# One core of T5 attention with a three-way maxout FFN: the left-over keys' band loaded by DMA, a spread moved to VectorE, bands and an FFN block reordered

## The chip, the cores and the metric

The kernel runs on one core of a Trainium2 chip. The metric is the device time of one execution in microseconds (us); less is better. The core has a matrix engine (TensorE, PE in the profile, with its weight loads as PEld), VectorE (DVE), ScalarE (ACT), GpSimd (POOL), a queue engine that only issues transfers (SyncE, SP), and 16 DMA engines. Each engine works through its own queue strictly in the order in which the program put it there. A semaphore makes an instruction wait for one on another engine, and everything behind it in its queue then waits too.

## The reference

Attention over 8 batches of 8 heads, 576 positions of 64 numbers, with a bias that depends on the distance of query and key alone; then an FFN whose hidden layer is the largest of three products.

```python
scores = scale * np.matmul(q, k.transpose(0, 1, 3, 2))
n = np.abs(pos[:, None] - pos[None, :])
bucket = np.where(n < half, n, large)            # large: logarithmic in n
scores = scores + bias_table[bucket].transpose(2, 0, 1)[None]
attn = softmax(scores)                           # over the keys
x = np.matmul(attn, v).transpose(0, 2, 1, 3).reshape(B * S, H * D)
h = np.maximum(np.maximum(x @ w1, x @ w2), x @ w3)
return h @ w_out                                 # 4608 x 512, w: 512 x 768
```

## The kernel before

Work goes by batch and, within a batch, by pair of heads (`hp` 0 to 3). For a pair, TensorE makes the scores with the keys on the partitions (tiles `sc`); ScalarE takes the exponential into `e4` (512 keys in 4 tiles, by 512 queries). The 64 left-over keys (positions 512 to 575; tile `sct`) and the 64 left-over queries (`scq`) go into a second tile, `el`. The bias is applied behind the exponential, as a factor: far from the diagonal it is constant and drops out in the division, so only a band around the diagonal is multiplied, on VectorE (`times_band`, `times_band_pair`, `times_band_left`, `times_bandt`). The factors stand in `hank`, 128 partitions by 8 heads by 384, where row p is the same vector shifted by p: a DMA with overlapping rows reads it from `w_dr`, a small vector per head in DRAM (`load_hank`, L340). The band is read backwards along the queries. For the left-over keys the rows of `hank` do not serve as they are, since the two heads of a pair share the 128 partitions: `bandt` holds their 192 factors per pair, made from `hank` by two GpSimd copies that also turn the order round (`make_bandt`, L356).

TensorE then multiplies `e4` and `el` by the values (tile `a`, two halves of the queries); VectorE divides by the sums (`quotients`: RECIPROCAL `rd`, then the product into `x_sb`). In batch one of eight, TensorE transposes `x_sb` (`xp`) and ScalarE copies it to `xT` (`x_transposes`), of which the FFN reads all four pairs' parts.

The batch that comes first (b = 0) is written out in two loops over `hp`. The first loop makes the scores of the first half of the queries for all pairs. The second makes the other half, and puts the weighted sums, quotients, bands and left-over work of earlier steps between them. `bands(hp)` multiplies the band of pair `hp`'s first half: one double and one single multiply. Behind these comes a general loop over (b, hp) from (1, 0) on.

The second batch (b = 1) is loaded in another layout, packed, into the end of `xT`, two heads first (`load_second`). `spread_packed(hp, engine)` copies a pair from there to `q_sb` and `k_sb`, one copy each; `second_transposes` then lets TensorE transpose them (10 transposes, `tp`), VectorE copies the queries to qT and ScalarE the keys to kT. For pair 0 the spread is done by GpSimd, for pairs 1 to 3 by VectorE.

The FFN is filler for TensorE. `add_ffn(t0, n)` appends the work on n tokens as a list of portions to `pending`, and `fill(target, ...)` takes portions from there while their sizes add up to no more than the target. For the first 256 tokens there are three blocks: `first(0)` (4), then `first(1)` with `second(0)` (8), then `second(1)` (4), then `first(2)` with `second(2)` (8). A `first` is 8 matmuls with the first weights and a ScalarE copy to `hT` (L418); a `second` is 8 matmuls with the second weights and a VectorE maximum (L427). The thirds follow later, deferred.

Of the kernel before, what the change touches and what calls it, by code (L numbers as in the profile page):

```python
# [12 lines left out]
ALU = mybir.AluOpType  # L13
# [26 lines left out]
def kernel(  # L40
# [12 lines left out]
    nc = tc.nc  # L53
    B, H, S, D = q.shape
# [5 lines left out]
    HP = H // 2  # L60
    QS = 2 * P
# [10 lines left out]
    BAND = 3 * P  # L72
    HALF = 2 * P - 1
    WL = 2 * HALF + 1
# [17 lines left out]
    inorder = tc.keep_in_program_order  # L92
# [19 lines left out]
    def tr(*args):  # L112
        inorder(nc.tensor.transpose(*args))  # L113
# [8 lines left out]
    def act_copy(out_, in_):  # L122
        return inorder(nc.scalar.activation(out=out_, in_=in_, func=ACTF.Copy))

    def dve_copy(out_, in_):
        return inorder(nc.vector.tensor_copy(out_, in_))  # L126
# [122 lines left out]
    def spread_packed(hp, eng):  # L249
        h = slice(2 * hp, 2 * hp + 2)  # L250
        for dst, src in zip(batch[1], (q_1, k_1)):
            inorder(eng.tensor_copy(dst[:, :, h, :], src[:, h].rearrange("p h t d -> p t h d")))
# [38 lines left out]
    for vv in range(single, NB):  # L291
# [5 lines left out]
        out=pick[:, 0:NW], in0=pick[:, 0:NW], scalar1=pick[:, NW:], scalar2=None, op0=ALU.is_equal,  # L297
# [38 lines left out]
    w_dr = dram.tile([H, WL], BF16, name="w_dr")  # L336
    hank = const.tile([P, H, BAND], BF16, name="hank")

    def load_hank(h0, h1):
        inorder(nc.sync.dma_start(  # L340
            out=hank[:, h0:h1, :],
            in_=bass.AP(
                tensor=w_dr.tensor, offset=w_dr.offset + h0 * WL,
                ap=[[1, P], [WL, h1 - h0], [1, BAND]],
            ),
        ))
# [2 lines left out]

    bandt = const.tile([P, HP, 192], BF16, name="bandt")  # L350

    def make_bandt():
        for par in range(2):
            r = slice(64 * par, 64 * par + 64)
            c = BAND // 2 - 64 * par
            inorder(nc.gpsimd.tensor_copy(bandt[r, :, :], hank[r, par::2, c : c + 192][:, :, ::-1]))  # L356

# [334 lines left out]
    def add_ffn(t0, nt, last=False):  # L694
        portions, left = ffn(t0, nt, last)
        portions[0] = rest + portions[0]
        rest[:] = left
        pending.extend((sum(n for n, _ in p), [fn for _, fn in p]) for p in portions)
# [10 lines left out]
    def fill(target, *hooks):  # L709

        groups, spent, hooks = [], 0, list(hooks)
        while pending and (not groups or spent + pending[0][0] <= target):
            n, fns = pending.pop(0)
            spent += n
            groups += [fn for fn in fns if fn]
        for j, group in enumerate(groups):
            while hooks and (j == len(groups) - 1 or j > 0 and len(hooks) > len(groups) - 1 - j):
                hooks.pop(0)()
            group()
        for hook in hooks:  # L720
            hook()
# [183 lines left out]

    def times_bandt(hp, el):
        return inorder(nc.vector.tensor_tensor(
            out=el[:, S - 192 : S], in0=el[:, S - 192 : S], in1=bandt[:, hp, :], op=ALU.mult
        ))

    def left_queries(hp, qT, kT, el):
# [113 lines left out]
    def x_transposes(hp, half):  # L1025

        xp = ps_f.tile([P, 2 * CH], BF16, tag="ff", name="xp")
        lo, hi = (0, QS) if half == 0 else (QS, S)
        for q in range(lo // P, -(-hi // P))[::-1]:
            c = min(P * q, S - P) - lo  # L1030
            tr(xp[:, c : c + P], x_sb[0][:, q, P * hp : P * hp + P], ident[:])
        act_copy(xT[:, hp, lo:hi], xp[:, 0 : hi - lo])
# [8 lines left out]
    def next_late():  # L1041
        return late.pop(0)() if late else (lambda: None)
# [13 lines left out]
    on_zeros(warm[:, 0:CH])  # L1056
    for h0 in (0, KT):
        load_hank(h0, h0 + KT)
    dve_copy(batch[0][0][:, 0:2, 2:KT, :], q32[:, :, 2:KT, :])
    cast_keys(1)  # L1060
    w_bf = [const.tile([P, DCH, d_ff], BF16, name=f"w{i}_bf") for i in range(3)]
# [10 lines left out]
    def load_second():  # L1072
        for h0, h1 in ((0, 2), (2, H)):
            load_packed(k, h0, h1, k_1)
            load_packed(q, h0, h1, q_1)
            if h0 == 0:
                load_q_tail(1)
                load_tail(k, 1, 0, H, k_diag)
                load_w(1)
                make_bandt()  # L1080
        spread_packed(0, nc.gpsimd)
        load_v(1, 0, H)
        load_w(2)

# [3 lines left out]
    def bands(hp):  # L1088
        times_band_pair(hp, first_e[hp], 0, 0)
        times_band(hp, first_e[hp], 2, 0, QS, inorder)  # L1090
# [9 lines left out]
    for hp in range(HP):  # L1100
        qT, kT = (x[:, hp, :] for x in qk[0])
        e4, el = e_tiles()
# [29 lines left out]
    for hp in range(HP):  # L1132
        qT, kT = (x[:, hp, :] for x in qk[0])
        if begun:
            e4, el = begun.pop()
            more_transposes(hp + 1)
            scores(qT, kT, e4, 1, 2)
        else:
            e4, el = e_tiles()
            visit(qT, kT, e4, [(1, 0), (1, 2)], (lambda: more_transposes(hp + 1)) if hp + 1 < HP else None)  # L1140

        def keys():
            left_keys(hp, qT, kT, el, QS, S)

        def queries():
            left_queries(hp, qT, kT, el)

        def late_bands(hp=hp, e4=e4):
            times_band(hp, e4, 1, QS, QM, inorder)
            times_band_pair(hp, e4, 2, QS)  # L1150

        if hp == 0:
            keys()
        if hp == 1:
            x_transposes(0, 0)
        quotients = next_late()
        if hp < 2:
            quotients()
            if hp == 0:
                bands(2)  # L1160
            else:
                behind.pop()()
                keys()
            queries()
            if hp == 1:
                x_transposes(1, 0)
            else:
                begun.append(e_tiles())
                scores(*(x[:, 1, :] for x in qk[0]), begun[0][0], 1, 0)
            quotients = next_late()  # L1170
            quotients()
            if hp == 0:
                bands(3)
            behind.append(lambda late_bands=late_bands, hp=hp, el=el: (late_bands(), products(hp, el)))
        else:
            if behind:
                behind.pop()()
            if hp == 3:
                quotients()
                add_ffn(0, QS)  # L1180
                fill(8)
            keys()
            if hp == 2:
                quotients()
            queries()
            late_bands()
            if hp == 2:
                x_transposes(2, 0)
                x_transposes(3, 0)
            else:  # L1190
                begin_qk(2)
                x_transposes(0, 1)
                fill(8, lambda: second_transposes(qk[1], 0))
            products(hp, el)
        late.append(lambda hp=hp, e4=e4, el=el: attend(0, hp, e4, el, 1))
# [15 lines left out]
    for b, hp in [(b, hp) for b in range(1, B) for hp in range(HP)]:  # L1211
# [3 lines left out]
        e4, el = begun[0] if begun else e_tiles()  # L1215
# [215 lines left out]
```

## Time and profile before

| quantity | before |
|---|---|
| time, median of 3 runs | 307.47 us (306.84 to 308.44) |
| profiled execution, its own time | 307.46 us |
| its span in the profile | 305.7 us |
| granted TensorE clock | 1.0 |
| GpSimd: two band copies (L356) | 2.1 us |
| GpSimd: the spread of pair 0 (L252) | 0.6 and 0.7 us |
| VectorE: a spread of pairs 1 to 3 (L252) | 333 ns (q), 283 ns (k), mean |

Times in the profile count from the start of its span. A row of the timeline gives the start, the time from the first start to the last end of the instructions that it merges, engine, line, operation, output and inputs; in brackets stands how long the engine idled just before, and the instruction that ended that. Instructions of one engine overlap a little, so the distance from start to start is less than the duration.

### The profile page before, as it was taken

The page shows a single profiled execution, that of the slowest core. Times are in us where ns is not written, and L with a number is a line of the kernel's source. Part 1 is how long each engine was busy: PE and PEld are TensorE (multiplying, and loading weights), DVE is VectorE, ACT ScalarE, POOL GpSimd, SP SyncE. Part 2 cuts the span into 40 slices and gives each one's busy share as a digit, 9 for nine tenths or more (in the row PEclk, how much of TensorE's full clock was granted, in tenths as well). Part 3 has the DMA queues.
Part 4 walks back from the last instruction along what each step waited for, and adds up shares of the span by engine and source line. Part 5 has one row for each costly group of instructions (what it writes and reads, how often), then busy time and mean ns, then how long its engine had stood idle before and what let it go on. Part 6 is the DMA issues. An engine that isn't in the chain of part 4 may idle for free.

```text
span 305.7 us, 10992 instructions
## 1 busy us (share of the span) xinstructions
PE 294.5 (96%) x4736; PEld 183.6 (60%) x4745; DVE 206.9 (68%) x455; ACT 201.3 (66%) x270; POOL 143.7 (47%) x199
## 2 busy tenths in 40 slices
PE   8778999999999999999999999999999999999995
PEld 2356878775556576667666766676667654444442
DVE  6489688787767767776777677767776765453552
ACT  3997998987786677768776877677777720222211
POOL 8998786725739655865686669460000000000000
PEclk9999999999999999999999999999999999999999
DMA  9999999999999999999999999999543013202003
GB/s 158 195 197 194 177 144 144 98 163 122 217 152 129 147 197 168 161 133 200 152 159 127 192 180 146 128 197 153 49 84 135 11 36 91 90 0 105 35 0 137
DMA packets 165777, 40.51 MB, mean 133 GB/s; under 512 B 154585, under 2 KB 161249, under 8 KB 165729
## 3 DMA queue, kind: packets, MB, share of 16 engines
q0 software_dynamic: 105664, 16.66, 96.6%
q1 hardware_dynamic: 58304, 22.69, 40.8%
q8 instruction: 37, 0.61, 0.9%
q10 hardware_dynamic: 1760, 0.47, 0.7%
q14 instruction: 12, 0.09, 0.2%
HBM read 35.39 MB, written 9.45 MB: 147 GB/s over the span
## 4 chain that ended last, share of the span: by engine, by line
PE 87%; ACT 6%; DVE 4%; issue 1%; DMA 1%; DVEq 0%; ACTq 0%
PE psp L109 36%; PE ps L109 17%; PE a L109 14%; PE sc L109 9%; PE pso L109 6%; ACT e L827 4%; PE sct L109 2%; PE warm L109 1%; PE scq L109 1%; DVE e L807 1%; ACT el L827 1%; DVE qT L126 1%; DMA out_dram<-osb 1%; DVE e L822 1%; PE tp L113 1%
## 5 line engine op out<-in xcount | busy, mean ns | idle before, releaser
L827 ACT ACTIVATE e<-sc 128x1024 bf16<-128x1024 f32 x128 | 129.0, 1026 | 29.6 <-PE sc L109 28.3
L109 PEld LDWEIGHTS <-w_bf 64*128 64x128 bf16 (+1 forms) x1112 | 75.9, 95 | 55.1 <-issue 1.5
L109 PE MATMUL psp<-xT,w_bf 64*128 64x512 bf16 x784 | 97.2, 376 | 0.0
L807 DVE TENSOR_TENSOR e<-e,hank 128x512 bf16<-128x512 bf16 (+2 forms) x120 | 57.7, 486 | 13.9 <-ACT e L827 13.2
L109 PE MATMUL ps<-xT,w_bf 128*128 128x512 bf16 (+1 forms) x324 | 58.9, 332 | 0.3
L109 PE MATMUL sc<-qT,kT 64*128 64x256 bf16 (+1 forms) x352 | 48.6, 319 | 2.4 <-ACT e L827 1.1
L199 POOL DMA_DIRECT2D k_sb<-in_k_dram x48 | 36.2, 768 | 18.3 <-DMA vx<-in_v_dram 10.6
L109 PE MATMUL a<-vx,e 64*128 64x65 bf16 (+1 forms) x1664 | 44.7, 190 | 0.0
L109 PEld LDWEIGHTS <-kT 64*128 64x128 bf16 (+1 forms) x712 | 30.1, 94 | 24.2 <-issue 7.1
L109 PEld LDWEIGHTS <-e 64*128 64x128 bf16 (+1 forms) x1664 | 40.7, 95 | 4.2
L199 POOL DMA_DIRECT2D q_sb<-in_q_dram x48 | 36.5, 771 | 11.9 <-DMA k_sb<-in_k_dram 3.0
L109 PEld LDWEIGHTS <-hT 64*128 64x128 bf16 (+1 forms) x462 | 28.2, 95 | 18.7 <-DVE hT L551 1.6
L167 POOL DMA_DIRECT2D vx<-in_v_dram x28 | 24.9, 899 | 23.0 <-DMA vx<-in_v_dram 9.3
L109 PE MATMUL psp<-wo_bf,hT 64*128 64x256 bf16 (+1 forms) x360 | 31.7, 305 | 0.0
L421 ACT ACTIVATE m<-ps 128x512 bf16<-128x512 f32 x14 | 8.4, 597 | 34.3 <-PE ps L109 34.3
L109 PEld LDWEIGHTS <-el 64*128 64x128 bf16 (+1 forms) x676 | 26.4, 94 | 7.0 <-issue 4.4
L827 ACT ACTIVATE el<-sct 128x576 bf16<-128x576 f32 (+2 forms) x36 | 21.7, 605 | 13.1 <-PE sct L109 13.0
L109 PE MATMUL a<-vt,el 64*128 64x65 bf16 (+1 forms) x260 | 29.6, 198 | 0.2 <-DVE m L511 0.2
L551 DVE TENSOR_TENSOR hT<-psp,m 128x1024 bf16<-128x1024 f32 (+1 forms) x20 | 18.7, 956 | 8.2 <-PE psp L109 8.2
L109 PE MATMUL pso<-wo_bf,hT 128*128 128x512 bf16 (+2 forms) x98 | 21.2, 366 | 0.2
L430 DVE TENSOR_TENSOR m<-ps,m 128x512 bf16<-128x512 f32 x14 | 9.7, 692 | 17.0 <-PE ps L109 17.0
L537 DVE TENSOR_TENSOR m<-psp,m 128x1024 bf16<-128x1024 f32 x15 | 18.4, 1224 | 3.3 <-PE psp L109 3.1
(82 smaller groups left out, 291.7 us busy)
## 6 DMA issues: line engine op xcount, KB each, us to landing
out_dram<-osb SPq DMA_DIRECT2D x35, 256.0 KB, 4.1
vx<-in_v_dram POOLq DMA_DIRECT2D x28, 128.0 KB, 6.3
q_sb<-in_q_dram POOLq DMA_DIRECT2D x50, 64.0 KB, 5.0
k_sb<-in_k_dram POOLq DMA_DIRECT2D x48, 64.0 KB, 4.8
w_bf<-in_moe_w_dram POOLq DMA_DIRECT2D x2, 512.0 KB, 8.5
xT<-in_k_dram SPq DMA_DIRECT2D x6, 128.0 KB, 4.6
hank<-w_dr SPq DMA_DIRECT2D x2, 384.0 KB, 4.8
w_bf<-in_moe_w_dram POOLq DMA_DIRECT2D x1, 768.0 KB, 8.4
```

The source lines that it names most:

```text
L109: made = inorder(nc.tensor.matmul(*args, **kw))
L113: inorder(nc.tensor.transpose(*args))
L126: return inorder(nc.vector.tensor_copy(out_, in_))
L167: in_turn(b, nc.gpsimd.dma_start(out=dst[:, t, h0:h1, :], in_=x[:, t, h0:h1, :]), P * (h1 - h0))
L199: in_turn(b, nc.gpsimd.dma_start(out=dst[:, g, :, par, :], in_=part), KT * P)
L421: nc.scalar.activation(out=st[fb]["m0"][:], in_=ps0, func=ACTF.Copy)
L430: inorder(nc.vector.tensor_tensor(out=m[:], in0=ps1, in1=st[fb]["m0"][:], op=ALU.max))
L537: return lambda: inorder(nc.vector.tensor_tensor(out=m[0][:], in0=ps1(), in1=m[0][:], op=ALU.max,))
L551: inorder(nc.vector.tensor_tensor(out=out_[:, i : i + n], in0=ps2()[:, i : i + n], in1=m[0][:, i : i + n], op=ALU.max,))
L807: put(nc.vector.tensor_tensor(out=e4[:, t, :, lo:hi], in0=e4[:, t, :, lo:hi], in1=hank[:, 2 * hp : 2 * hp + 2, c0:c1][:, :, ::-1], op=ALU. ...
L822: inorder(nc.vector.tensor_tensor(out=e4[:, t : t + 2, :, lo : lo + n], in0=e4[:, t : t + 2, :, lo : lo + n], in1=band, op=ALU.mult,))
L827: made = nc.scalar.activation(out=out_, in_=in_, func=ACTF.Exp, scale=inv_sqrt_d)
```

## The change

Four edits go together.

- `bandt` is loaded by two DMAs on SP's queue, from `w_dr`, right behind the two `hank` loads. It is stored in the forward order, and `times_bandt` reads it backwards. The two GpSimd copies are gone.
- Pair 0 of the second batch is spread by VectorE in place of GpSimd: at the end of the second loop's last step, ahead of `second_transposes`.
- In the second loop's first step, `bands(2)` is issued ahead of the quotients.
- `add_ffn(0, QS)` moves from the second loop's last step to the end of the step before it, with a `fill(4)`. Both `fill(8)` of the last step stay, and so take the portions that came one call later before.

```diff
-    def make_bandt():
+    def load_bandt():
         for par in range(2):
-            r = slice(64 * par, 64 * par + 64)
-            c = BAND // 2 - 64 * par
-            inorder(nc.gpsimd.tensor_copy(bandt[r, :, :], hank[r, par::2, c : c + 192][:, :, ::-1]))
+            inorder(nc.sync.dma_start(
+                out=bandt[64 * par : 64 * par + 64, :, :],
+                in_=bass.AP(
+                    tensor=w_dr.tensor, offset=w_dr.offset + par * WL + BAND // 2,
+                    ap=[[1, 64], [2 * WL, HP], [1, 192]],
+                ),
+            ))
...
-            out=el[:, S - 192 : S], in0=el[:, S - 192 : S], in1=bandt[:, hp, :], op=ALU.mult
+            out=el[:, S - 192 : S], in0=el[:, S - 192 : S], in1=bandt[:, hp, :][:, ::-1], op=ALU.mult
...
         load_hank(h0, h0 + KT)
+    load_bandt()
...
                 load_w(1)
-                make_bandt()
-        spread_packed(0, nc.gpsimd)
         load_v(1, 0, H)
...
         quotients = next_late()
+        if hp == 0:
+            bands(2)
         if hp < 2:
             quotients()
-            if hp == 0:
-                bands(2)
-            else:
+            if hp:
                 behind.pop()()
...
             if hp == 3:
                 quotients()
-                add_ffn(0, QS)
                 fill(8)
...
                 x_transposes(2, 0)
                 x_transposes(3, 0)
+                add_ffn(0, QS)
+                fill(4)
             else:
                 begin_qk(2)
                 x_transposes(0, 1)
+                spread_packed(0, nc.vector)
                 fill(8, lambda: second_transposes(qk[1], 0))
```

Three places show what this does to the queues. First VectorE in the second loop's first step, before; `e4_289` is pair 2, `e4_318` pair 3, `a_390` and `a_432` are the sums of pairs 0 and 1.

```order
L126 COPY qT_189<-tp2_376 128x320
L962 RECIPROCAL rd_409<-a_390 128x4
L963 TENSOR_TENSOR x_sb_223<-a_390,rd_409 128x2x128
L822 TENSOR_TENSOR e4_289<-e4_289,hank_187 128x4x256
L807 TENSOR_TENSOR e4_289<-e4_289,hank_187 128x2x128
L962 RECIPROCAL rd_451<-a_432 128x4
L963 TENSOR_TENSOR x_sb_223<-a_432,rd_451 128x2x128
L822 TENSOR_TENSOR e4_318<-e4_318,hank_187 128x4x256
L807 TENSOR_TENSOR e4_318<-e4_318,hank_187 128x2x128
L126 COPY qT_189<-tp2_456 128x320
```

The same place of the change; pair 2 is now `e4_291`, pair 3 `e4_320`.

```order
L126 COPY qT_189<-tp2_374 128x320
L826 TENSOR_TENSOR e4_291<-e4_291,hank_187 128x4x256
L811 TENSOR_TENSOR e4_291<-e4_291,hank_187 128x2x128
L966 RECIPROCAL rd_409<-a_388 128x4
L967 TENSOR_TENSOR x_sb_225<-a_388,rd_409 128x2x128
L966 RECIPROCAL rd_449<-a_430 128x4
L967 TENSOR_TENSOR x_sb_225<-a_430,rd_449 128x2x128
L826 TENSOR_TENSOR e4_320<-e4_320,hank_187 128x4x256
L811 TENSOR_TENSOR e4_320<-e4_320,hank_187 128x2x128
L126 COPY qT_189<-tp2_454 128x320
```

The two multiplies of pair 2 stand ahead of the quotients of pair 0; the rest is as it was.

Second, VectorE at the end of the second loop, before: `x_sb` of the sums `a_629`, the bands of pair 3's other half (`e4_615`), then the copy of batch two's transposed queries, and the maximum of `second(0)` (`ps1_729`).

```order
L963 TENSOR_TENSOR x_sb_223<-a_629,rd_657 128x3x128
L807 TENSOR_TENSOR e4_615<-e4_615,hank_187 128x2x128
L822 TENSOR_TENSOR e4_615<-e4_615,hank_187 128x4x256
L126 COPY qT_191<-tp_714 128x512
L126 COPY qT_191<-tp_714 128x64
L427 TENSOR_TENSOR hT_660<-ps1_729,hT_660 128x512
```

And in the change, where the maximum of `second(0)` is that of `ps1_679`, and that of `second(1)` is `ps1_739`:

```order
L967 TENSOR_TENSOR x_sb_225<-a_638,rd_666 128x3x128
L431 TENSOR_TENSOR hT_611<-ps1_679,hT_611 128x512
L811 TENSOR_TENSOR e4_624<-e4_624,hank_187 128x2x128
L826 TENSOR_TENSOR e4_624<-e4_624,hank_187 128x4x256
L252 COPY q_sb_222<-xT_101 128x4x128
L252 COPY k_sb_223<-xT_101 128x4x128
L126 COPY qT_191<-tp_724 128x512
L126 COPY qT_191<-tp_724 128x64
L431 TENSOR_TENSOR hT_611<-ps1_739,hT_611 128x512
```

The maximum of `second(0)` moved from behind the transposes' copy to ahead of the bands, and the two spread copies stand between the bands and that copy.

Third, ScalarE over the same stretch, before: the copies of `x_sb`'s transposes to `xT`, the exponentials of pair 3 and of its left-over part, and the copies of `first(0)` (`ps0_661`) and `first(1)` (`ps0_704`).

```order
L827 ACTIVATE el_537<-scq_593 128x2x4x64
L123 ACTIVATE xT_101<-xp_605 128x256
L123 ACTIVATE xT_101<-xp_609 128x256
L827 ACTIVATE e4_615<-sc_617 128x2x2x256
L827 ACTIVATE e4_615<-sc_623 128x2x2x256
L418 ACTIVATE hT_660<-ps0_661 128x512
L827 ACTIVATE el_616<-sct_671 128x320
L827 ACTIVATE el_616<-scq_674 128x2x4x64
L123 ACTIVATE xT_101<-xp_699 128x320
L418 ACTIVATE hT_660<-ps0_704 128x512
L123 ACTIVATE kT_192<-tp_714 128x512
```

And in the change, where `first(0)` is `ps0_612` and `first(1)` is `ps0_669`:

```order
L831 ACTIVATE el_535<-scq_591 128x2x4x64
L123 ACTIVATE xT_101<-xp_603 128x256
L123 ACTIVATE xT_101<-xp_607 128x256
L422 ACTIVATE hT_611<-ps0_612 128x512
L831 ACTIVATE e4_624<-sc_626 128x2x2x256
L831 ACTIVATE e4_624<-sc_632 128x2x2x256
L422 ACTIVATE hT_611<-ps0_669 128x512
L831 ACTIVATE el_625<-sct_689 128x320
L831 ACTIVATE el_625<-scq_692 128x2x4x64
L123 ACTIVATE xT_101<-xp_717 128x320
L123 ACTIVATE kT_192<-tp_724 128x512
```

Each block's copy moved ahead of a pair of exponentials, as its matmuls did on TensorE. In batch two's first step, TensorE had `second(1)` at the first `fill` and `first(2)`, `second(2)` at the next one, behind the transposes of pair 1; now the first `fill` takes `first(2)` and `second(2)`, and nothing is pending at the next.

## The prediction

> **What bounds the kernel now.** I read the page's busy shares first, then the chain of work that ended last, then busy time by stretches, and last the timeline of the stretches that the change touches.
>
> ```profile
> span 305.7 us, 10992 instructions
> PE 294.5 (96%) x4736; PEld 183.6 (60%) x4745; DVE 206.9 (68%) x455; ACT 201.3 (66%) x270; POOL 143.7 (47%) x199
> ...
> PE 87%; ACT 6%; DVE 4%; issue 1%; DMA 1%; DVEq 0%; ACTq 0%
> ...
> 16.00:24.00 8.00, 5.20 (x106) 3.98 (x103) 6.47 (x16) 6.74 (x12) 6.98 (x11) 1.00 1.59 186
> 24.00:30.00 6.00, 5.67 (x111) 4.25 (x107) 5.90 (x20) 5.41 (x9) 5.87 (x8) 1.00 1.41 199
> 30.00:36.00 6.00, 6.00 (x87) 4.67 (x85) 4.01 (x11) 5.56 (x12) 3.91 (x6) 1.00 2.03 171
> 48.00:60.00 12.00, 11.69 (x196) 9.33 (x193) 9.37 (x26) 11.15 (x18) 7.83 (x12) 1.00 2.08 111
> ```
>
> In the stretches the first columns are length, then busy PE, PEld, DVE, ACT, POOL. TensorE is busy in 96% of the span. It idles 2.80 us of 16 to 24, 0.33 us of 24 to 30, and nothing of 30 to 36. So a microsecond that TensorE loses or gains before 42 reaches the end, unless a later wait swallows it; 48 to 60 has only 0.31 us of such waits. Note ACT at 5.56 of 6 and 11.15 of 12: nearly full too. What counts is therefore when TensorE gets through each place, and whether ScalarE and VectorE, which work their queues in order, have its input ready.
>
> **The band copies and the earlier bands: a gain of 1.53.**
>
> ```profile
> 18.78 0.18 DVE L962 RECIPROCAL rd<-a 128x4 f32<-128x4 f32 x1 [1.37 <-PE a L109]
> 20.09 0.91 DVE L807 TENSOR_TENSOR e<-e,hank 128x256 bf16<-128x256 bf16 x1
> 21.07 2.13 POOL L356 COPY bandt<-hank 64x768 bf16<-64x768 bf16 x2
> 21.47 1.03 DVE L822 TENSOR_TENSOR e<-e,hank 128x1024 bf16<-128x1024 bf16 x1
> 21.80 0.29 PE L109 MATMUL scq<-qT,kT 64*128 64x64 bf16 x8 [0.16 <-ACT e L827]
> 22.43 0.91 DVE L807 TENSOR_TENSOR e<-e,hank 128x256 bf16<-128x256 bf16 x1
> 23.62 0.27 PE L113 MATMUL xp<-ident,x_sb 128*128 128x128 bf16 x2 [1.53 <-DVE qT L126]
> ...
> 30.26 0.28 DVE L807 TENSOR_TENSOR e<-e,hank 128x256 bf16<-128x256 bf16 x1
> 30.46 0.68 DVE L822 TENSOR_TENSOR e<-e,hank 128x1024 bf16<-128x1024 bf16 x1
> ```
>
> TensorE's one long stall is the 1.53 us before 23.62. It waits for VectorE's qT copy, which stands behind three band multiplies. These took 0.91, 1.03 and 0.91 us around GpSimd's two band copies; the same forms take 0.28 and 0.68 at 30.3. So 0.63 + 0.35 + 0.63 = 1.61 us of VectorE's time there goes with those copies. (The page calls GpSimd's spans rough, so that the first of the three begins ahead of the recorded copies says little.) The change deletes them, and moves the first two multiplies into the 1.37 us in which VectorE waited before 18.78 (even if the first 0.63 had another cause, it would now be hidden). The qT copy comes 1.6 us sooner, and TensorE follows its scq block without a pause: 23.62 - 1.53 = 22.09. ScalarE idled after that scq block too, so it moves along. On GpSimd's queue the loads behind the deleted copies issue up to 3 us sooner; TensorE waits for no load in these stretches, so I take nothing for that.
>
> What replaces the copies is two loads behind the hank loads on SP's queue, which holds nothing more until the batch-three transposes.
>
> ```profile
> L340 SPq DMA_DIRECT2D hank<-w_dr x2: 371/439/507, 11.0 to 11.4; - x2
> DMA to landing us min/median/max: 4.0/4.8/5.6
> ...
> L907 DVE TENSOR_TENSOR el<-el,bandt x32: 243/251/259, 24.8 to 244.2; 128x192 bf16<-128x192 bf16 x32
> L920 DVE TENSOR_TENSOR el<-el,hank x3: 214/218/218, 25.0 to 29.4; 128x128 bf16<-128x128 bf16 x3
> ```
>
> Each holds a quarter of a hank load's bytes. Issued by about 12.5 and landing within the 5.6 us of the slowest hank load they are there at 18; the first use, at 24.8 before, comes near 23.3. I take nothing for them; they cost from the moment they land 5 us late. Reading the band backwards costs nothing: a reversed read of 128 elements takes 218 ns and of 256 takes 280, and the forward 192 lies between at 251. From -0.03 to +0.03 us in each of 32, off the path.
>
> **The first FFN block sooner: the new wait A.** It now stands right behind the transposes of x_sb into xT for the third and fourth head pairs.
>
> ```profile
> 27.07 0.40 PE L113 MATMUL xp<-ident,x_sb 128*128 128x128 bf16 x4
> 27.40 0.82 PE L109 MATMUL sc<-qT,kT 64*128 64x256 bf16 x8
> 27.67 0.65 ACT L123 ACTIVATE xT<-xp 128x256 bf16<-128x256 bf16 x2
> ...
> 32.37 0.87 PE ps L109 x8
> 33.24 0.54 PE sc L109 x8
> ...
> 34.06 0.90 PE a L109 x27
> ```
>
> (The last three are of the chain, which gives net times.) The block multiplies xT, so it needs both ScalarE copies, done at 27.67 + 0.65 = 28.32. Before, TensorE went on at 27.40 with scores that need no such copy. Now it stands from 25.87 (27.40 - 1.53) to 26.83 (28.32 - 1.53 + 0.04 of signalling): A = 0.96 us. Nothing can hide it, since ScalarE's copies stand behind its exps as before.
>
> **The spread on VectorE: the new wait B.** The second half of block 0 (`second(0)`) also moves ahead, and its maximum now stands in VectorE's queue before the bands of the fourth pair and the two spread copies, for which the batch-two transposes wait.
>
> ```profile
> 31.65 0.39 PE L113 MATMUL tp<-ident,q_sb 128*128 128x128 bf16 x4
> 32.21 1.04 PE L109 MATMUL ps<-xT,w_bf 128*128 128x256 bf16 x8
> 33.18 0.61 PE L109 MATMUL sc<-qT,kT 64*128 64x256 bf16 x8
> 33.35 0.69 DVE L427 TENSOR_TENSOR hT<-ps,hT 128x512 bf16<-128x512 f32 x1 [0.15 <-PE ps L109]
> 33.96 0.25 DVE L907 TENSOR_TENSOR el<-el,bandt 128x192 bf16<-128x192 bf16 x1
> ...
> 36.72 0.28 DVE L252 COPY q_sb<-xT 128x512 bf16<-128x512 bf16 x1
> 36.92 0.29 DVE L252 COPY k_sb<-xT 128x512 bf16<-128x512 bf16 x1
> 43.75 0.43 DVE L252 COPY q_sb<-xT 128x512 bf16<-128x512 bf16 x1
> ```
>
> TensorE from 26.83: `first(0)` 0.87, sc 0.54, a 0.90, `first(1)` 0.87; `second(0)` starts at 30.01. Its maximum starts 1.14 us after it (32.21 to 33.35), at 31.15. Start to start the maximum takes 0.61 (33.35 to 33.96), the single band 0.20 (30.26 to 30.46), and the double one about 0.60. The q copy starts at 32.56 and ends at 32.84, and the transposes start at 32.88. TensorE alone would be ready near 31.5 (0.87 for the block and some 0.65 for two small score blocks and xp), so B is about 1.4 us. From the transposes to the first scores of batch two it was 33.18 - 31.65 = 1.53 us with one FFN block between, and still is: 34.41. That is 1.23 us late against 33.18, with one block of 0.87 done ahead.
>
> **The missing filler: the new wait C.** Pulling everything one step ahead leaves the end of batch two's first step with no FFN block.
>
> ```profile
> 36.01 0.39 PE L109 MATMUL sc<-qT,kT 64*128 64x256 bf16 x4
> 37.89 1.04 ACT L827 ACTIVATE e<-sc 128x1024 bf16<-128x1024 f32 x1
> 38.48 1.91 PE L109 MATMUL ps<-xT,w_bf 128*128 128x256 bf16 x16
> 39.12 0.81 ACT L123 ACTIVATE kT<-tp 128x512 bf16<-128x512 bf16 x2
> 40.32 0.61 PE L109 MATMUL sc<-qT,kT 64*128 64x256 bf16 x8
> ```
>
> Before, TensorE finished the transposes at 38.48 and spent 1.84 us on two blocks (x16) until 40.32, while ScalarE, behind its exp of 37.89, copied kT until 39.93. Now the two blocks come earlier in the step, one of them in place of the one that is already done: the scores that stood at 36.01 start at 34.41 + (36.01 - 33.18) + 0.87 = 38.11. From there to the end of the kT copy ScalarE needs 39.93 - 36.01 = 3.92 as before, so the next scores start at 42.07 with 0.04 of signalling. TensorE would have been there near 40.6; C is about 1.4 us.
>
> **The sum.** 42.07 against 40.32 is +1.75 us, with the same blocks done. (In parts: -1.53, A +0.96, B +1.4, C +1.4, and the remaining -0.5 are small waits of TensorE between 27 and 41 in the run of before, which the new ones contain.) Behind this place the order of every compute engine is unchanged and TensorE full. The profiled execution took 307.46, which is the median of the runs shown (307.47): 307.46 + 1.75 = **309.2 us**.
>
> GpSimd's rows give a price for a collision of the new spread with its DMA issues.
>
> ```profile
> L199 POOL DMA_DIRECT2D q_sb<-in_q_dram x48 | 36.5, 771 | 11.9 <-DMA k_sb<-in_k_dram 3.0 <-DMA vx<-in_v_dram 3.0 <-DMA vt<-in_v_dram 2.4
> ```
>
> Of the quoted spread copies one took 0.43 in place of 0.28, so I keep 0.15 as the usual end of that and 0.77, one whole issue, as the other. The Trainium skill, "SBUF — State Buffer", section "Who interferes with whom", says that a VectorE copy in a two-port mode and GpSimd exclude each other for a whole instruction. By that rule the copy could wait out an issue, and the sum would be 310.0; the quoted copies have not shown a wait of that length.
>
> **Rivals.**
> - *The filler isn't missed* (22%): ScalarE, freed of the hT copy that stood behind kT, has kT ready when TensorE arrives, and C is nothing. Then 309.2 - 1.4 = 307.8, no change. For it: the copy of the early blocks falls into ScalarE's idle time. Against: kT stands behind an exp that starts only after the scores, and 3.92 us is longer than TensorE's 2.5.
> - *ScalarE's pace decides, not TensorE's place* (7%), the faster side: ScalarE is 5.56 of 6 busy from 30 to 36, and if its exps run on through A and B, only the 1.53 is left: 305.9. It decides at the kT copy, which would have to end by 38.4. Against: the exps of the fourth pair are queued behind the block's hT copy, so they wait for A as well.
> - *The spread collides with GpSimd's issues* (15%), at B: +0.77, 310.0; the band loads landing late ends there too.
> - That the band isn't read, or the copies stay, can't be: the instructions are gone.
>
> **How the numbers follow.** The forecast has 56%, with 0.6 to each side for the rounding of three waits. 0.5% of 307.47 (about what a measurement of this kernel tells from no change) puts the bounds at 305.9 and 309.0. Slower by more: the collision's 0.15 and 0.38 of the 0.56 make 0.53. Faster: 0.06. Within: 0.41. The range 307.4 to 310.4 holds the forecast, the rival at 307.8 and the one at 310.0; the faster one is left out.
>
> **What would show it.** In the changed profile: band multiplies of 0.28 and 0.68 near 20, and no wait of TensorE for qT at 22; a wait of ps for ScalarE's xT near 25.9 of about 1 us (A); of tp for VectorE's q_sb near 31.5 of 1.2 to 1.4 us (B); of sc for ScalarE's kT near 40.6 of 1.2 to 1.5 us (C). I am wrong if TensorE reaches the second pair's scores of batch two before 41, or if the lateness there is won back between 42 and 100.

## The result, and the profile after

The changed kernel takes 309.03 us (median of 14 runs, 308.28 to 310.46); the kernel before, on the same chip beside it, 306.80. The ratio is 1.0062, with a 95% interval of 1.0037 to 1.0086: about 1.9 us slower (the two medians as such lie 2.2 us apart). A second measurement (the experiment `after_again`) gave 1.0047 (1.0026 to 1.0069), about 1.4 us.

The profiled execution of the change took 310.46 us, the longest of its 14, so its places need care. First its page and the list of TensorE's waits (engine, line, releaser: us in total, times, longest):

```profile
span 308.7 us, 10999 instructions
PE 295.8 (96%) x4745; PEld 183.8 (60%) x4745; DVE 204.9 (66%) x457; ACT 201.7 (65%) x270; POOL 140.7 (46%) x195
...
PE tp L113 <- DVE q_sb L252: 1.2, 1, 1.2
PE sc L109 <- ACT kT L123: 1.1, 1, 1.1
PE ps L109 <- ACT xT L123: 0.6, 1, 0.6
```

The span is 3.0 us longer than before's 305.7. The wait for qT that headed the list (1.53 us) is gone; three new ones stand in its place, and all are those of the prediction: `ps` for xT (A), `tp` for q_sb (B), `sc` for kT (C). The timeline of the same execution shows each in its place (start, duration, what ran, and the idle time before it with its releaser):

```profile
10.94 0.48 PE L113 MATMUL tp<-ident,ktail 128*128 128x128 bf16 x3 [0.74 <-DMA ktail<-in_k_dram]
15.96 0.28 PE L113 MATMUL tp<-ident,q_sb 128*128 128x128 bf16 x2
23.12 0.29 PE L113 MATMUL xp<-ident,x_sb 128*128 128x128 bf16 x2
26.58 0.40 PE L113 MATMUL xp<-ident,x_sb 128*128 128x128 bf16 x4
27.18 0.65 ACT L123 ACTIVATE xT<-xp 128x256 bf16<-128x256 bf16 x2
27.61 1.03 PE L109 MATMUL ps<-xT,w_bf 128*128 128x256 bf16 x8 [0.63 <-ACT xT L123]
33.79 0.40 PE L113 MATMUL tp<-ident,q_sb 128*128 128x128 bf16 x4 [1.23 <-DVE q_sb L252]
42.85 0.61 PE L109 MATMUL sc<-qT,kT 64*128 64x256 bf16 x8 [1.10 <-ACT kT L123]
```

The first row, a wait for `ktail`, is on a load of the first 11 us that the change does not touch. Two executions are best laid side by side at a place that lies behind the early loads and ahead of what the change touches on TensorE: the small block of query transposes, `tp` x2, at 15.96 here. In the profile of before it stands at 14.87:

```profile
14.87 0.28 PE L113 MATMUL tp<-ident,q_sb 128*128 128x128 bf16 x2
```

So 1.09 us of the lateness are there before the first changed instruction on TensorE. I call this `tp` the **mark**, and the second pair's scores of batch two (`sc` x8 with the wait C) the **place**. From mark to place it is 40.32 - 14.87 = 25.45 us before and 42.85 - 15.96 = 26.89 us after: the change costs 1.44 us here (1.75 were forecast). From the place to the end of the span it is 305.7 - 40.32 = 265.4 before and 308.7 - 42.85 = 265.9 after, so nothing is won back.

The band multiplies of VectorE between 16 and 28 us (groups by form: busy, mean ns of one, idle before), the two band loads on SP's queue, and busy time by stretches (length, then PE, PEld, DVE, ACT, POOL):

```profile
L826 DVE TENSOR_TENSOR e<-e,hank 128x1024 bf16<-128x1024 bf16 x7 | 4.8, 681 | 0.0
L811 DVE TENSOR_TENSOR e<-e,hank 128x256 bf16<-128x256 bf16 x7 | 2.0, 282 | 0.0
...
L911 DVE TENSOR_TENSOR el<-el,bandt x32: 238/251/259, 24.3 to 247.4; 128x192 bf16<-128x192 bf16 x32
L354 SPq DMA_DIRECT2D bandt<-w_dr x2: 683/888/1092, 11.3 to 12.0; - x2
DMA to landing us min/median/max: 7.0/7.2/7.4
...
30.00:36.00 6.00, 4.77 (x64) 3.63 (x61) 3.94 (x10) 3.95 (x9) 2.96 (x5) 1.00 1.93 175
```

No multiply is slowed any more: 0.68 and 0.28 throughout. The reversed read has the same median as the forward one, 251 ns. The loads land near 19.5, later than expected but well ahead of the first use at 24.3. And TensorE, which was full from 30 to 36, now idles 1.23 us there.

### The profile page after: what moved, and what is told of

The parts are those of the page before. It is cut to its first block, busy times and chain, and to the rows that moved or that the text cites. A ratio compares the mean times of both kernels' runs of the same rounds, so it can differ in the third digit from the quotient of the medians.

```text
span 308.7 us, 10999 instructions
## 1 busy us (share of the span) xinstructions
PE 295.8 (96%) x4745; PEld 183.8 (60%) x4745; DVE 204.9 (66%) x457; ACT 201.7 (65%) x270; POOL 140.7 (46%) x195
## 4 chain that ended last, share of the span: by engine, by line
PE 87%; ACT 6%; DMA 3%; issue 1%; DVE 1%; POOL 1%; DVEq 0%; POOLq 0%; ACTq 0%
PE psp L109 36%; PE ps L109 17%; PE a L109 13%; PE sc L109 9%; PE pso L109 6%; ACT e L831 4%; PE sct L109 2%; DMA ktail<-in_k_dram 2%; PE scq L109 1%; ACT el L831 1%; PE tp L113 1%; DMA out_dram<-osb 1%; POOL q_sb L167 0%; ACT xT L123 0%; PE idle L109 0%
## 5 line engine op out<-in xcount | busy, mean ns | idle before, releaser
L811 DVE TENSOR_TENSOR e<-e,hank 128x512 bf16<-128x512 bf16 (+2 forms) x120 | 56.1, 472 | 14.1 <-ACT e L831 13.4
```

The lines of the kernel that those rows point to most:

```text
L811: put(nc.vector.tensor_tensor(out=e4[:, t, :, lo:hi], in0=e4[:, t, :, lo:hi], in1=hank[:, 2 * hp : 2 * hp + 2, c0:c1][:, :, ::-1], op=ALU. ...
```

## The experiments

All ratios below are to the kernel before, run beside. "Place" is the distance from mark to place in the profile, and "rest" the time from the place to the end of the span. Both are read from one profiled execution of each kernel. The intervals of many neighbours overlap, so what a single edit is worth is read from the place and not from the ratio.

| kernel | ratio (95% interval) | place | rest |
|---|---|---|---|
| before | 1 | 25.45 | 265.4 |
| the change | 1.0062 (1.0037 to 1.0086) | 26.89 | 265.9 |
| `after_again`: the change | 1.0047 (1.0026 to 1.0069) | 27.00 | 265.4 |
| `ffn_only` | 1.0072 (1.0037 to 1.0107) | 26.95 | 265.6 |
| `filler_split` | 1.0044 (1.0023 to 1.0066) | 26.36 | 265.5 |
| `behind_scores` | 1.0033 (1.0007 to 1.0059) | 26.31 | 266.9 |
| `spread_on_pool` | 1.0029 (1.0007 to 1.0051) | 25.74 | 265.5 |
| `bands_only` | 0.9999 (0.9970 to 1.0028) | 24.71 | 266.0 |
| `ffn_late` | 0.9994 (0.9972 to 1.0015) | 23.87 | 268.5 |
| `ffn_late_wo` | 1.0012 (0.9983 to 1.0042) | 23.89 | 267.2 |
| `band_dma_only` | 0.9966 (0.9931 to 1.0000) | 23.87 | 268.3 |
| `dma_bands` | 0.9986 (0.9960 to 1.0011) | 23.87 | 268.1 |
| `less_v_before` | 0.9969 (0.9940 to 0.9999) | 24.12 | 265.6 |
| `less_v_ffn_late` | 0.9946 (0.9924 to 0.9969) | 23.96 | 265.7 |

### The FFN block back in its place: `ffn_late`

```diff
             if hp == 3:
                 quotients()
+                add_ffn(0, QS)
                 fill(8)
...
                 x_transposes(3, 0)
-                add_ffn(0, QS)
-                fill(4)
```

> The change without its last edit: the first FFN block is where it was before, in the second loop's last step; band by DMA, bands sooner and the spread on VectorE stay. Theory: waits A, B and C all hang on the FFN block's move, so all three go and the stall of 1.53 us before xp stays away: 1.5 us below the kernel before, ratio 0.995 (0.9935 to 0.9965). In the trace tp<-q_sb waits less than 0.2 us, ps and sc wait for no xT or kT copy. Rival 1, the spread on VectorE costs by itself (0.5 us of VectorE's queue ahead of the transposes): 0.5 us less gain, ratio 0.997. Rival 2, the 1.53 us are swallowed by a later wait: ratio 1.000.

Measured: ratio 0.9994. The timeline of TensorE, the mark, the place, and its two long waits for loads behind it:

```profile
14.47 0.28 PE L113 MATMUL tp<-ident,q_sb 128*128 128x128 bf16 x2
38.34 0.61 PE L109 MATMUL sc<-qT,kT 64*128 64x256 bf16 x8
...
67.46 1.46 PE L109 MATMUL pso<-wo_bf,hT 128*128 128x512 bf16 x6 [0.98 <-DMA wo_bf<-in_moe_w_out_dram]
91.59 0.30 PE L109 MATMUL sct<-qT,kT 64*128 64x288 bf16 x2 [0.58 <-DMA kT<-ktail]
```

Up to the place the theory holds to a tenth: 23.87 us in place of 25.45, A, B and C gone, and the spread on VectorE costs nothing (rival 1 falls). But rival 2 decides the time: the ratio shows nothing of the 1.58 us. The profiled execution, the longest of the 12 (308.59; the shortest took 305.87), loses them and more. Its rest is 268.5 us, 3.1 more than before's, and TensorE waits for the output weights and for a transposed kT, neither of which it waited for in either profile above. These two waits are 1.56 of the 3.1; the remainder was not traced.

### The spread back on GpSimd: `spread_on_pool`

```diff
                 load_w(1)
+        spread_packed(0, nc.gpsimd)
...
                 x_transposes(0, 1)
-                spread_packed(0, nc.vector)
```

> The change with the spread of batch two's first pair back on GpSimd, behind the loads; all else as changed. Theory: wait B (1.23 us in the trace, tp for VectorE's q_sb) goes, A (0.63) and C (1.10) stay: 1.2 us below the changed kernel, ratio to the kernel before 1.002 (1.001 to 1.0035). Rival, B only stands in the place of C or of ScalarE's pace, which takes its time again if B goes: same as the changed kernel, ratio 1.006, with a C of about 2.3 us. Second rival, the spread on GpSimd slows VectorE's bands as the band copies did: 0.3 to 0.6 us of the 1.2 lost, ratio 1.004.

Measured: ratio 1.0029. Mark, `tp` and place:

```profile
14.92 0.28 PE L113 MATMUL tp<-ident,q_sb 128*128 128x128 bf16 x2
31.55 0.38 PE L113 MATMUL tp<-ident,q_sb 128*128 128x128 bf16 x4
40.66 0.61 PE L109 MATMUL sc<-qT,kT 64*128 64x256 bf16 x8 [1.10 <-ACT kT L123]
```

The `tp` follows without a wait and the place comes at 25.74, 1.15 us ahead of the change's 26.89, while C stays at 1.10. B is the spread's own, and worth its full length. Only together, though: with the FFN block late, the spread on VectorE costs nothing (`ffn_late` and `dma_bands`, which differ in it alone, both have 23.87). It is the block's maximum ahead of it in VectorE's queue that makes it late.

### A filler kept: `filler_split`

```diff
-portions = [[f[0]], [f[1], m[0]], [m[1]], [f[2], m[2]]]
+portions = [[f[0]], [f[1], m[0]], [m[1]], [f[2]], [m[2]]]
...
-        rate = 8 if b == 1 or (b, hp) == (2, 0) else 13
+        rate = 4 if (b, hp) == (1, 0) else 8 if b == 1 or (b, hp) == (2, 0) else 13
...
-                fill(8, lambda: second_transposes(qk[1], 0))
+                fill(4, lambda: second_transposes(qk[1], 0))
```

> The change with its FFN blocks portioned so that batch two's first step keeps one block of 0.87 us for each of its two fills (first(2) at the first, second(2) at the second, behind the transposes of the next pair). All that is computed is the same. Theory: C is a missing filler; a block of 0.87 us stands where TensorE waited 1.10, and the second scores come 0.6 to 0.9 us sooner: ratio to the kernel before 1.003 to 1.004, A and B as in the changed kernel, sc's wait for kT 0.5 us or less. Rival, ScalarE's pace decides there and the block moved only makes the earlier scores come sooner into a longer wait: ratio 1.006.

Measured: ratio 1.0044.

```profile
14.92 0.28 PE L113 MATMUL tp<-ident,q_sb 128*128 128x128 bf16 x2
41.28 0.61 PE L109 MATMUL sc<-qT,kT 64*128 64x256 bf16 x8 [0.56 <-ACT kT L123]
```

C falls from 1.10 to 0.56, and the place comes 0.53 us sooner (26.36): a little less than expected. A missing filler is what C is, but one block of 0.87 us takes only half of it away. The other 0.3 us go on ScalarE: the block's copy to `hT` (0.63 us, from 37.39 on) now stands in ScalarE's queue ahead of the exponential of the pair's first scores. That exponential starts 0.75 us behind those scores (37.12 to 37.87), in the change 0.43 (39.05 to 39.48), and the copy of kT stands behind it.

### The block's move alone: `ffn_only`

> The kernel before with the FFN block's move alone; GpSimd's band copies, its spread and the bands' order as before. Theory: A (0.6 to 1.0 us) and C (1.1 to 1.4) come, B does not since GpSimd has spread the pair long before; the stall of 1.53 before xp stays. Less the small waits of before that they contain (0.5): 1.2 to 2.0 us above the kernel before, ratio 1.004 to 1.0065. Rival, the moved block alone is harmless and all of the change's loss is the spread's wait B: ratio 1.000.

The edit is the inverse of `ffn_late`'s, made to the kernel before. Measured: ratio 1.0072.

```profile
14.86 0.28 PE L113 MATMUL tp<-ident,q_sb 128*128 128x128 bf16 x2
23.24 0.27 PE L113 MATMUL xp<-ident,x_sb 128*128 128x128 bf16 x2 [1.16 <-DVE qT L126]
27.72 1.03 PE L109 MATMUL ps<-xT,w_bf 128*128 128x256 bf16 x8 [0.63 <-ACT xT L123]
41.81 0.61 PE L109 MATMUL sc<-qT,kT 64*128 64x256 bf16 x8 [1.10 <-ACT kT L123]
```

A and C come with the move alone. Without the stall of 1.16 it would stand at 26.95 - 1.16 = 25.79, where `spread_on_pool` stands (25.74). One detail was not expected: the stall for qT is 1.16 here, not 1.53, though nothing ahead of it differs from the kernel before. Two of the three band multiplies ahead of the qT copy show why:

```profile
20.07 0.91 DVE L807 TENSOR_TENSOR e<-e,hank 128x256 bf16<-128x256 bf16 x1
21.45 0.68 DVE L822 TENSOR_TENSOR e<-e,hank 128x1024 bf16<-128x1024 bf16 x1
```

The double multiply took 0.68, not 1.03, and that is the difference; GpSimd's copies are recorded from 21.45 on here, from 21.07 in before's profile. The single one of 0.91 ended (20.98) ahead of the copies, and so it did in before's profile (21.00 against 21.07). That its 0.63 us belong to the copies is thus not shown by the rows. It ran beside the issue of a load of w_bf (19.97 to 21.50), but beside the same issue in `band_dma_only` (21.07 to 22.58) this form took 0.28.

### The band by DMA alone, and the bands' order alone: `band_dma_only`, `bands_only`, `dma_bands`

These take the parts of the diff as they are: the two loads with the reversed read; `bands(2)` ahead of the quotients; and both of these together.

> The kernel before with bandt loaded by DMA (and read backwards) as the only edit; bands, spread and FFN as before. Theory: GpSimd's copies slowed three band multiplies by 0.63 + 0.35 + 0.63 us; all go to 0.28 and 0.68, the qT copy starts near 21.6 and TensorE goes on from scq without its stall of 1.53. The second pair's first scores of batch two, counted from the tp at 14.87, come 1.5 us sooner (23.9 in place of 25.45). The time: as much of that as the loads behind it let through, ratio 0.995 to 1.000. Rival, the earlier bands are needed as well: 0.6 to 1.0 us of the stall go, 24.5 to 24.9. Second rival, something else slowed the multiplies: stall and place as before.

> The kernel before with the third pair's bands ahead of the quotients as the only edit; GpSimd's copies stay. Theory: the first two multiplies go into VectorE's idle time, the other two still meet GpSimd's copies and take 1.0 and 0.9; the qT copy comes about 0.7 us sooner, the stall of 1.53 falls to about 0.8, and the second pair's first scores of batch two, counted from the tp at 14.87, come 0.7 us sooner (24.75 in place of 25.45). Ratio 0.997 to 1.000. Rival, the order is all that counts: stall gone, 23.9. Second rival, GpSimd's copies slow whatever stands beside them and the order gives nothing: stall 1.3 to 1.5.

> The change without the FFN block's move and with the spread of batch two's first pair on GpSimd: band by DMA and bands sooner alone. Theory: same as band_dma_only at 41 us, since without GpSimd's copies the bands' order wins nothing more: second scores of batch two 23.9 us behind the tp at 14.87; time 0.996 to 0.9995 of the kernel before, with waits for DMA between 65 and 120 in TensorE's rows. Rival, the earlier bands win 0.3 to 0.6 us more: 23.3 to 23.6.

`band_dma_only`, ratio 0.9966; TensorE:

```profile
14.80 0.28 PE L113 MATMUL tp<-ident,q_sb 128*128 128x128 bf16 x2
38.67 0.61 PE L109 MATMUL sc<-qT,kT 64*128 64x256 bf16 x8
...
76.25 1.04 PE L109 MATMUL psp<-xT,w_bf 64*128 64x512 bf16 x8 [0.83 <-DVE e L811]
113.74 0.39 PE L109 MATMUL sc<-qT,kT 64*128 64x512 bf16 x2 [1.96 <-DMA kT<-k_sb]
```

`dma_bands`, ratio 0.9986 (mark at 14.91):

```profile
38.78 0.61 PE L109 MATMUL sc<-qT,kT 64*128 64x256 bf16 x8
77.32 1.04 PE L109 MATMUL psp<-xT,w_bf 64*128 64x512 bf16 x8 [1.58 <-DMA xT<-x_sb]
```

The DMA edit alone brings the whole 1.58 us, and the order nothing more on top of it: 23.87 both times. Both then meet waits of 1.6 to 2.0 us for DMA transposes later on.

`bands_only`, ratio 0.9999; GpSimd's copies, and TensorE:

```profile
14.34 0.28 PE L113 MATMUL tp<-ident,q_sb 128*128 128x128 bf16 x2
22.36 1.92 POOL L356 COPY bandt<-hank 64x768 bf16<-64x768 bf16 x2
24.63 0.23 PE L109 MATMUL a<-vt,el 128*128 128x130 bf16 x1 [0.93 <-DVE el L907]
39.05 0.61 PE L109 MATMUL sc<-qT,kT 64*128 64x256 bf16 x8
```

The place moves by 0.74 us against before's profile, the 0.7 expected, but not for the reason given. The stall for qT is wholly gone, and another one of 0.93 us stands at 24.63: the left-over multiply waits for `bandt` itself, which GpSimd finished only at 24.28. In this execution the copies ran 1.3 us later than in that of before (22.36 against 21.07), so the new order and the later copies are not told apart by it.

### A cure for the lost gain that did not work: `ffn_late_wo`

```diff
                 load_v(b + 1, 0, H)
+                if b == 1:
+                    load_last_weights()
                 load_pair(b + 1, 2)
...
-            if b == 1:
-                load_last_weights()
             load_pair(b + 1, 3)
```

> The kernel of ffn_late (first FFN block where it was before, the rest as changed), and the load of the output weights (wo_bf) issued ahead of the third pair's loads of the next batch, in place of behind them. Theory: in ffn_late the 1.5 us were won up to 41 us and then given back at TensorE's first output product, which waited 0.98 us for wo_bf (issued at 57.5, landed 9.9 us later), and at kT from ktail (0.58). With wo_bf loaded some 5 us sooner that wait goes, and more of the gain reaches the end: ratio to the kernel before 0.9955 to 0.9975. Rival, the loads as a whole set the pace there, and the pair pushed behind wo_bf makes another wait of the same length (a transposed kT or qT): ratio 0.999 to 1.001.

Measured: ratio 1.0012 (mark at 14.26).

```profile
38.15 0.61 PE L109 MATMUL sc<-qT,kT 64*128 64x256 bf16 x8
76.14 1.04 PE L109 MATMUL psp<-xT,w_bf 64*128 64x512 bf16 x8 [1.22 <-DMA xT<-x_sb]
```

The wait for wo_bf is gone, and one of 1.22 us for the DMA transpose of x_sb is there instead. The rival holds: it isn't one late load.

### The first block behind the scores: `behind_scores`

```diff
                 x_transposes(3, 0)
-                add_ffn(0, QS)
-                fill(4)
...
+        if hp == 3:
+            add_ffn(0, QS)
+            fill(4)
         quotients = next_late()
```

> The change with the first FFN block's first(0) behind the scores of the second loop's last step in place of ahead of them; all later fills as changed. Theory: A (0.63 us in the trace) goes, since the scores need no xT copy and cover ScalarE's two copies; B and C stay at 1.2 and 1.1. The time is 0.6 us less than the changed kernel's: ratio to the kernel before 1.004 (1.003 to 1.005). Rival, B takes it back, since VectorE's maximum comes no sooner when ScalarE's copy of the block stands behind the exponentials: ps waits for nothing, tp waits 1.8, ratio 1.006.

Measured: ratio 1.0033.

```profile
14.48 0.28 PE L113 MATMUL tp<-ident,q_sb 128*128 128x128 bf16 x2
26.17 1.05 PE L109 MATMUL ps<-xT,w_bf 128*128 128x256 bf16 x8
31.72 0.40 PE L113 MATMUL tp<-ident,q_sb 128*128 128x128 bf16 x4 [1.23 <-DVE q_sb L252]
40.79 0.61 PE L109 MATMUL sc<-qT,kT 64*128 64x256 bf16 x8 [1.10 <-ACT kT L123]
```

`ps` waits for nothing, B and C keep their lengths, and the place comes 0.58 us sooner (26.31 against 26.89). A is worth about the 0.63 of its row.

### The change again, and fewer loads: `after_again`, `less_v_before`, `less_v_ffn_late`

> The changed kernel once more, for a second profile. Theory: the wait of TensorE for ktail near 10.9 us and the dip of the clock in the first profile are not the change's: here the tp that stood at 15.96 stands within 0.6 us of the 14.87 of before, A, B and C are 0.6, 1.2 and 1.1 again, and the second pair's first scores of batch two stand 26.9 us behind that tp (25.45 before). Ratio 1.006. Rival, the two band loads on SP's queue delay the early loads: ktail again late by about 1 us.

```profile
14.42 0.28 PE L113 MATMUL tp<-ident,q_sb 128*128 128x128 bf16 x2
41.42 0.61 PE L109 MATMUL sc<-qT,kT 64*128 64x256 bf16 x8 [1.10 <-ACT kT L123]
```

The mark stands at 14.42, ahead of before's, with no wait for ktail: the 1.09 us of the first profile were not the change's. The place is 27.00, B 1.34 here.

For the other two, one edit, made to the kernel before and to `ffn_late`:

```diff
-            if b < 3:
-                load_v(b + 1, 0, H)
-                load_pair(b + 1, 2)
-            else:
-                load_pair(b + 1, 2, lambda t: load_main(v, b + 1, 0, H, vx[(b + 1) % 2][:, :, :, 0:D], t, t + 1))
-                load_tail(v, b + 1, 0, H, v_diag)
+            load_pair(b + 1, 2)
```

> The kernel before without the loads of the values of batches two to seven (counted from 0): those batches use the values of batches 0 and 1. A base for less_v_ffn_late: 4.7 MB of 40.5 are not moved, all else is as before. Theory: TensorE sets the time here, so it is little changed: ratio to the kernel before 0.996 to 1.000.

> The kernel of ffn_late without the loads of the values of batches two to seven, as in less_v_before. Theory: the 1.5 us that ffn_late wins up to 41 us are given back between 65 and 120 since the loads and DMA transposes go at a pace of their own, about 1 to 2 us behind TensorE; with a tenth of the bytes gone they are ahead, and the gain reaches the end: 1.5 us less than less_v_before (0.995 of it), TensorE's waits for DMA between 60 and 130 below 0.5 us in sum. Rival, the gain goes elsewhere (ScalarE's or TensorE's own pace): same time as less_v_before, and as little DMA wait.

Both leave out values that the result needs, so they are probes and not versions to use. The bytes saved were 40.51 - 36.97 = 3.5 MB, less than the 4.7 expected. Ratios 0.9969 and 0.9946. `less_v_before` first, with GpSimd's copies and the xp that stalled before, then the place of `less_v_ffn_late` (mark at 14.24):

```profile
14.62 0.28 PE L113 MATMUL tp<-ident,q_sb 128*128 128x128 bf16 x2
21.76 1.78 POOL L356 COPY bandt<-hank 64x768 bf16<-64x768 bf16 x2
21.84 0.27 PE L113 MATMUL xp<-ident,x_sb 128*128 128x128 bf16 x2
38.74 0.61 PE L109 MATMUL sc<-qT,kT 64*128 64x256 bf16 x8
```

```profile
38.20 0.61 PE L109 MATMUL sc<-qT,kT 64*128 64x256 bf16 x8
```

For the stretch behind the place the theory holds. `less_v_ffn_late` reaches the place as early as `ffn_late` (23.96 and 23.87), and its rest is 265.7 us where that of `ffn_late` was 268.5; the list of TensorE's waits has no DMA in either kernel with fewer loads. So the loads and transposes are what takes the early kernels' gain, or GpSimd's issuing of those loads, which goes with them. The times fit: the nine executions of `less_v_ffn_late` took 305.65 to 306.62, the twelve of `ffn_late` 305.87 to 308.59. For the gain itself the pair is a miss: I expected 0.995 between them and the two differ by 0.38 us in the median (305.98 and 306.36), and the profiled execution of `less_v_before` didn't have the stall at all. Its xp at 21.84 stands as if no copy disturbed it, although its queues up to there are those of the kernel before. The copies began 0.7 us later than in before's profile (21.76 against 21.07), behind the multiplies that this xp hangs on. The multiplies that they then met, of 0.57 and 1.34 us from 22.25 on, stood on a stretch where TensorE waited only 0.29 us for them.

## Why the prediction was right, and where not

The time was 309.03 for 309.2 forecast, and the three new waits are the right ones. That the two times agree to 0.2 us is in part luck. The sum started from 307.46, the median of three runs, and the kernel before has 306.80 in fourteen; with +1.75 that gives 308.55. And the distance from mark to place grew by 1.44 in one profile and 1.55 in the other, for 1.75 forecast. Point by point:

- **The band copies, -1.53**: in this profile -1.59 (mark to xp: 23.62 - 14.87 = 8.75 before, 23.12 - 15.96 = 7.16 after). That it goes with the copies is shown by `band_dma_only`, which brings all of it; for the first of the three multiplies, how they slow it stays open (see `ffn_only`). What the prediction could not know from one execution is that the stall is no fixed price: with the same queues ahead of it, it was 1.53, 1.16 and nothing in three executions. The copies wait in GpSimd's queue behind loads, so they fall on the band multiplies or beside them. Before's profile reaches the place at 25.45, that of `less_v_before`, with the same queues up to there, at 24.12. What the copies cost on the average of the executions is thus not known; of the three seen, 1.53 is the longest.
- **The earlier bands**, which the prediction books together with the copies, add nothing to the DMA edit (23.87 with and without). The 0.63 us that the prediction let VectorE's idle time hide would have been saved either way.
- **A, +0.96**: the right wait, mis-sized. From xp to ps it is 27.61 - 26.58 = 1.03 where before the scores followed xp by 27.40 - 27.07 = 0.33, so A is 0.70. The prediction let the block wait for both copies; the row shows ps starting at 27.61, before the second one ended (27.18 + 0.65 = 27.83). These 0.26 us with the signalling are the whole error. That the block's first matmuls read the parts copied earlier is argued from this, not tried apart.
- **B, +1.4**: 1.23 in the trace, 1.15 as the difference that `spread_on_pool` makes. The path named, a maximum and the fourth pair's bands ahead of the spread, is the one seen, and the block's place and the spread are needed both.
- **C, +1.4**: 1.10. From `tp` to the second scores it was to be 42.07 - 32.88 = 9.19 us, and is 42.85 - 33.79 = 9.06. The same reading error as in A is in it: the scores start at 42.85, before the second of the two kT copies had ended (42.15 + 0.81 = 42.96). And TensorE arrived later: it needed 2.70 us from the first scores (39.05) to the wait, not 2.5.
- **The remaining -0.5** is wrong. It was to be small waits of TensorE between 27 and 41 in the run of before. TensorE idles 0.03 us there (busy 13.97 of 14.00), and the prediction's own row has it at 6.00 of 6 from 30 to 36. The measured parts need no such term: -1.59 + 0.70 + 1.23 + 1.10 = 1.44, which is the whole distance. The three waits were put 0.7 too long in sum, and the -0.5 hid most of that. The forecast did not rest on it, since 42.07 was worked out along the path, and that path was 0.3 too long.
- **The loads** were called landed by 18; they landed near 19.5 (7.2 us in place of 4.8), and it cost nothing, as said. "Loads behind the deleted copies issue up to 3 us sooner" did not come: GpSimd then waited for running transfers instead. Its next issue moved from 23.99 before to 24.62 after, even counted from the mark 0.5 us sooner and not 3:

```profile
24.62 0.83 POOL L247 DMA_DIRECT2D xT<-in_k_dram  x1 [1.26 <-DMA w_bf<-in_moe_w_dram]
```

- **"A microsecond that TensorE loses or gains before 42 reaches the end"**: true for the loss, false for the gain. In the profiles, kernels that reach the place at 25.4 or later have a rest of 265.4 to 265.9 (one has 266.9, with a gap of 1.32 us at 117 that its trace gives no releaser for). Those that reach it at 23.9 with all loads have 267.2 to 268.5. How much of the gain is lost differs by execution: three of these four profiles are of the longest or second longest of 12. By their ratios the four kernels lie at 0.9966 to 1.0012, 0.9990 in the mean, so about 0.3 of the 1.58 us arrive on average, by an estimate whose single ratios are uncertain by 0.002 to 0.0035 each. Here the sum was a loss, so the error did no harm; a forecast of the good half alone, 1.5 us faster, would have been wrong by it.
- The rivals: C came, so the filler was missed. ScalarE's pace did not decide. The spread's collision with GpSimd's issues was missing in the first profile (0.28 and 0.29 us for the two copies) and small in the second, where the q copy met a load's issue (31.60 to 32.22) and B was 1.34:

```profile
31.91 0.40 DVE L252 COPY q_sb<-xT 128x512 bf16<-128x512 bf16 x1
```

In `ffn_late` this copy took 0.48 and in `ffn_late_wo` 0.58, where it delayed nothing; none was longer by a whole issue of 0.77. The Trainium skill, in "SBUF — State Buffer", "Who interferes with whom", has the second one to come wait out the whole instruction of the first. These rows don't show such a wait: in `ffn_late` the k copy of 0.28 (from 29.23 on) ran beside issues of loads that fill 26.54 to 30.06. Whether these copies run in the mode that the rule is for isn't shown.

No version that loads everything beats the kernel before beyond doubt. `band_dma_only` comes nearest, and its interval ends at 1.0000.

## What to carry to other kernels

Here TensorE was full; a loss on it reached the end, and a gain reached it only as far as the transfers behind it ran ahead. In such a kernel look, further down the profile, for how long before its use each load lands. Moving a filler block ahead opened a gap where it had stood, and put its follow-up work (here a maximum) ahead of what shares that queue. A merged row's end is not what a reader of its first part waits for: A and C were both put too long by that. A stall between two engines whose timing hangs on transfers can differ from execution to execution; see it in a second profile before counting it.

## What was not expected of the hardware

- GpSimd's two band copies together took 2.13, 2.24, 1.92 and 1.78 us in four executions (one copy alone 0.83, with VectorE idle beside it in `bands_only`). How long they take does not follow from the multiplies beside them: the 1.78 were with two slowed multiplies (0.57 and 1.34), the 1.92 with none.
- The two band loads behind the hank loads took 7.0 to 7.4 us to land, and the hank loads' median rose from 4.8 to 6.8 us beside them; the four share SP's queue. In the second profile they took 6.5 to 6.8, and the hank loads 5.6.
- In the first profile of the change the granted clock of TensorE was 0.91 over the first 20 us (0.66 from 10 to 15), in the same stretch as the late ktail load; in the second it was 1.00. Which of the two brought how much of the 1.09 us was not separated.
